# Later attention groups without selector matmuls, and one MLP chunk per batch, in an attention plus MLP kernel

## The chip, the cores and the metric

The kernel runs on one core of one Trainium2 chip. The metric is the time of one execution on the device in microseconds; before the change it is 378.05 us, the median of three runs (377.97 to 380.45). The engines are named as in the profile: PE is TensorE (PEld its weight loads), DVE is VectorE, ACT is ScalarE, POOL is GpSimd, SP is SyncE, which issues most of the DMAs.

## The reference

Eight batches of eight heads of linear attention, 576 positions of 64 numbers, feed an MLP over 4608 tokens.

```python
def phi(x):                                  # x: [b, h, 576, 64], w_phi: [64, 128]
    proj = einsum('bhsd,df->bhsf', x, w_phi)
    proj = proj - max(abs(proj), axis=-1)    # one maximum per position and head
    return concatenate([exp(proj), exp(-proj)], axis=-1)

q_p, k_p = phi(q), phi(k)
kv  = einsum('bhsf,bhsd->bhfd', k_p, v)
z   = sum(k_p, axis=2)
num = einsum('bhsf,bhfd->bhsd', q_p, kv)
den = einsum('bhsf,bhf->bhs', q_p, z) + 1e-06
x   = (num / den) transposed to [4608, 512]

h = x @ w_in                                 # [512, 2048]
g = where(h > 0, h, exp(min(h, 0)) - 1)
out = g @ w_out                              # [2048, 512], fp32
```

Because proj has its maximum m taken off before both signs, the two halves are exp(p - m) and exp(-p + m) with the same m: the first half is scaled by exp(-m), the second by exp(+m).

## The kernel before

Sixteen groups of four heads (two per batch, `n` = 0 to 15) go through the attention. For each, k and q are turned so that the 64 head dimensions lie on partitions (two pairs of heads on the two halves of 128), by PE for the first four groups and by DMA transposes afterwards. The maximum for k scales v (on POOL). The maximum for q has to come off inside the exponent, and there the positions lie along the free axis: so the maxima, found in another layout, are split into two bf16 parts, transposed on PE, and added to the projection by "selector" matmuls.

```python
def m_max(n, c):                   # maxima of |q projection|, from PSUM, on DVE
    ...
    nc.vector.tensor_reduce(mq, st["pm", n, c][:, :, 0:p1 - p0, :], axis=AX.X, op=ALU.max, ...)

def m_split(n, part):              # hi and lo parts of the maxima
    ...
    eng = nc.gpsimd if n < PE_TRANSPOSED else nc.vector
    eng.tensor_copy(hi, mq)
    eng.tensor_tensor(mhl[n % 2][:, :, NI + p[0]:NI + p[1]], mq, hi, op=ALU.subtract)

def m_pe(n, part, bank=None):      # one transpose of them
    nc.tensor.transpose(tr[:, 0, :], mhl[n % 2].rearrange("p r x -> p (r x)"), ident)

def m_copy(n, part):
    nc.vector.tensor_copy(st["mT", n], st["trm", n][:, 0:1, :])

def q_mm(n, c, bank=None):
    ...                            # the projections, w_sb against qT: 2 matmuls a piece
    for j in range(w):             # the selectors: 6 matmuls a piece
        for par in range(2):
            nc.tensor.matmul(places(par, j, 1), sel[rows, p0 + j, :], mT[rows, 0, :],
                             start=False, stop=(j == w - 1))

def q_exp(n, c, sg):               # exp(+-(p - m)) on ACT, 768 columns
    ...
def x_mm(n, part, bank=None):      # both signs accumulated in one place: num and den
    ...
        nc.tensor.matmul(pn[:, hi, x, :], Eq[:, sg, hi, par, ...], kv_sb[:, hi, pr, sg, :],
                         start=(sg == 0), stop=(sg == 1))

def x_div(n, part):
    nc.vector.tensor_scalar_add(den, pn[:, :, :, D], 1e-6)
    nc.vector.reciprocal(rec, den)
    nc.vector.tensor_tensor(xp..., pn[:, :, :, 0:D], rec..., op=ALU.mult)
```

The result is turned once more into `xT_sb`, one tile of 4608 columns that stays in SBUF, by DMA transposes from group 2 on (`x_dma`: 512 columns of whole tiles, and 64 of a mixed one per batch). The columns of two batches and their mixed tile lie one after the other, and the MLP takes them 512 at a time, nine chunks: `h_mm` (w_in against x, L510), `h_exp` on ACT (L521), `h_min` on POOL (L526), `h_elu` on DVE (L530), `o_mm` (g against w_out, L538), `o_copy` on ACT (L548), `o_store` (L554).

All eight PSUM banks are one tile; each step is told its bank. The whole program is written out as a string of letters, one per step, and is issued in that order on every engine:

```python
ORDER = """
eabefegcj7dfkA0gj7BfkBeA2CA4hBl7gl6Bmj1mj0hBCM6iBkkA2DCBFEl1NDA4Bl0EmBOCFP1BEA6QBmS2CEM0CTU4eNDB
... (22 more lines)
"""
STEPS = dict(
    c=(selectors, [()]), d=(selectors2, [()]), e=(load k), f=(load q), g=(load v),
    j=(t_pe k), k=(t_copy k), l=(t_pe q), m=(t_copy q), n=(t_dma k), o=(t_dma q),
    A=(k_mm), B=(k_exp), C=(k_max), D=(v_exp), E=(v_scale), F=(v_ones),
    M=(m_mm), N=(m_max), O=(m_split), P=(m_pe), Q=(m_copy), S=(q_mm), T=(q_exp),
    U=(kv_mm), V=(kv_copy), W=(x_mm), X=(x_div), Y=(x_pe), Z=(x_copy), z=(x_dma),
    p=(h_mm), q=(h_exp), r=(h_min), s=(h_elu), t=(o_mm), u=(o_copy), v=(o_store))   # arguments cut
```

Of the kernel before, what the change touches and what calls it, by code (L numbers as in the profile page):

```python
# [10 lines left out]
FP32 = mybir.dt.float32  # L11
# [7 lines left out]
eabefegcj7dfkA0gj7BfkBeA2CA4hBl7gl6Bmj1mj0hBCM6iBkkA2DCBFEl1NDA4Bl0EmBOCFP1BEA6QBmS2CEM0CTU4eNDB  # L19
EUTOEM6VM0DP3NW4EQNM6S2NM0OTFENU6TXP1FOUQS2VP5Y4Tj1ZS6QTl0W4mTS2kTj0XTW6TkS4XA0Tj3BY2ZA6Tkl2Bp3m  # L20
Y5BCqBZrA0p4sCM2qp5rNM6qDrBNp3l2sqp7BmrsqM4rp6NFp2qsqrp5srp4CqOqrP7l3srW0sgQmp6sEj7XqS2DTrEkM0p5
NY7qTsrS0sFp4EZTsM2M6TNp5EqNS0qrp3Trp2sOsTA6fp4CqU0qrrUBssVqA2Bp5rW0sBP7p6Xqnt4qrBrsp1QCp5zqp7qr
sp0qrszW2DsrqFsS5rEp1sTXp7qp0Trfsp3qA1rtBesqp7ECoqp6qtDrBrsp5rzsqEp0sqS1qztTrrsFTsp7EU5uS1qrUrTs
A3Vt0TCtsBW1oW5BXp7A3qtCzrtsBXzt7BnM1A5M3NBtuCztDFNEM0BztNgM2uvt6ODENP7M0nM4QNES2tTNFTfS0S4TEA2t
CTp7TTU0UBA4VtBCp1qorBW2sqp0vBOXrp7quP5p4rzQsDqFW2sqrzp6XrA0qEp5szBsp3rqCvp7rqseBp4vsrqp6DsrqS0s
rM2Tp5NFEqp7sqrp3qrsTp4rsqsM0qA5rt2CEp7NBrtsBsM0qS5NtrTEsTS0U3oTA5UCTtVBt7OnBP4W0QuS3XvW5TtDXzTE
tztfFA0EuzS2M4Bt6NTztCTS4BM2otDTEtzTFA0Eut7CntNgBA4BM2CtNtBBA0OU2CUDuP6p5VQM2qM6Np4rNEp3qBsW6rqp
2sBrp5XqFeW0qsrzS6DXrp4TEzTp3sqEsvM0S6Np2TFnEqS0Tp5rqrsU6qzrUsTrp4TzOsp3qVorA0qsA6p2Brsvsp5qCP4r
p3qQCBrp4qsW0qrst2DXBEp5BFsW0zrqtEszXS6rtTvsM0A3NtBnTt5CztDBFEM0S6zNM3TtENTU0guA3S6UTotVBvt2BtTC
p1OA3qW6urp0XBP5tBQztqCzS5uA3t7DCTEntsDBFtrBEsW1TtXEA3uM5ep0NzBEp7Cqvp6rBFsM1qp5NqrM3qrS0Np2Trsf  # L30
p4qsTp7rqOsp6qrsP5rS0qQsU2oTrUsTS4Vvp7TsW0TzS2qXA4p6rBgTzp1Cqt0svqrTp7rszDW2sBEp6Xqp5rqzstrqsrA1
S3M6EsTotCFtNDt5BEtBETM6U1NFA3UBM6VtuNBvW0tCnXA6M2Bt4NBtCW0tODXuEp7vP6EA0QM2BtzNfqp6Cuzrp5BzS2qM
0Dt4rNTzFtETssvS0EU2TS6qtFoOTrtTesUTA0nVp5uCW2zqP7p6BXrvgp4BQsqzS2qA0rp7CTrzp5sqBsrp6Dsp4BEqM0qp
7NrTrsW0qsqA2rp5BXEp6BsFqp1rCqrp4sDrqsS2rp7sTEsqA5t0BrTtCFEqU1sBrUA3sS5BtVoTCtTzA1Bt7CuzW3DBEtXn
BtEDM0M2zFNW4EtXFt6nEuNM0U4vOM2NUP7tNtQVS0M2S4TNp7TOtTt3TqS0A4rop2BTtCvTtszqA0BrtCzup7sDBzp6qW4r
qvp2uXEBp3rqszA0qM4rsp7FNzrp6qECvp5sBrp4sqsp2qrDrqP7p3Qsqrp7BsrsqS5qA0srp4Brst2EqsBp3FTECp7qtrTr
sqtsrM0U4sUNA6tBVM0BS3Nt5CtODtTFEW0uP7TtEQXS2uA6t4TzCtBzW0BtXDTFtEzW0uEp7XzS2U4TzUTS0Vvt6qTrS2vT
p5Tzp4TW0qp3XqrtrqszW0rp7Xzp2qszp1rsqtsrqzsp5rsvp7sp4p3tp2uqp1vqrqt6rsqp0rsqrsqtrsqp7rsrsp5qsp4r
qsp3rqstrqsp7rstqp5rsp4qp7rqst3rqsp5rstqtrstp7t5qp4rsp2qtrqsp7rsp4qtrqsp2rstqp7rsp4qut2ruvsqp6rv
tqsutrvstt7ttp6p5qtrqsp4rst6qtrsp5tqp4rsp3qp5rqsp1rqsutrqvsut4ruvsttvtt7p6p5qtrqsup3rvstqp6rstp5  # L40
uqp4vqrp7qrsp3rsqst6rqstrsttt7utvttt6utvttt7utvttuv
# [4 lines left out]
def kernel(  # L46
# [34 lines left out]

    consts = ctx.enter_context(tc.tile_pool(name="consts", bufs=1))
# [5 lines left out]
    moep = ctx.enter_context(tc.tile_pool(name="moep", bufs=2))  # L88
    epool = ctx.enter_context(tc.tile_pool(name="epool", bufs=4))
# [24 lines left out]
    xT_sb = consts.tile([P, N_CT, NTOK], BF16)  # L114
    FULL = 4 * P

    def full_col(b):
        return (b // 2) * 2 * S + (b % 2) * (FULL + P)

    def mixed_col(b):  # L120
        return (b // 2) * 2 * S + FULL + (b % 2) * D

    def out_rows(tile_index):
        bp, t = divmod(tile_index, 9)
        rows = []
        for half in range(2):
            if t == 4:
                b, s = 2 * bp + half, 8
            else:
                b, t4 = (2 * bp, t) if t < 4 else (2 * bp + 1, t - 5)  # L130
                s = 4 * (t4 // 2) + t4 % 2 + 2 * half
            rows.append(
                out[b * S:(b + 1) * S, :].rearrange("(p s) c -> s p c", s=NS)[s]
            )
        return rows
# [11 lines left out]
    PIECES = (((0, 4), (4, 7), (7, 9)), ((0, 3), (3, 6), (6, 9)))  # L147
    TILES = (
# [56 lines left out]


# [12 lines left out]
    def t_copy(name, n, j0, j1):  # L219
        nc.vector.tensor_copy(  # L220
            get((name + "T", n), new_t(name))[:, j0:j1, :],
            st["tr", name, n, j0][:, 0:j1 - j0, :],
        )

    def t_dma(name, n):
        nat = st[name, n // 2][:, 2 * (n % 2):2 * (n % 2) + 2]
        nc.sync.dma_start_transpose(
            out=get((name + "T", n), new_t(name)),
            in_=nat.rearrange("p r s d -> p (r s d)"),
        )  # L230
# [56 lines left out]
    def m_mm(n, c, bank=None):  # L287
        own = min(n // FIRST, 1)
        p0, p1 = PIECES[own][c]
        pj = two_banks(bank).rearrange("p r (i f) -> p r i f", f=F)  # L290
        for j in range(p1 - p0):
            for par in range(2):
                rows = slice(par * D, (par + 1) * D)
                nc.tensor.matmul(  # L294
                    pj[:, par, j, :],
                    st["qT", n][rows, PLACE_OF[own][par][p0 + j], :],
                    w_sb[rows, :],
                    start=True,
                    stop=True,
                )  # L300
        st["pm", n, c] = pj

    def m_max(n, c):
        p0, p1 = PIECES[min(n // FIRST, 1)][c]
        if n < FIRST and c == 0:

            mq = st["pm", n, c][:, 0, 0, 0:2 * p1].rearrange("p (r i) -> p r i", r=2)
            st["mq0", n] = mq
        else:
            mq = get(("mq", n), lambda: small.tile([P, 2, NI], FP32, name="mq"))  # L310
            mq = mq[:, :, p0:p1]
        nc.vector.tensor_reduce(  # L312
            mq, st["pm", n, c][:, :, 0:p1 - p0, :], axis=AX.X, op=ALU.max,
            apply_absolute_value=True,
        )

    def m_split(n, part):
        if n < FIRST:
            p = ((0, 4), (4, NI))[part]
        else:  # L320
            p = (0, NI)
        hi = mhl[n % 2][:, :, p[0]:p[1]]
        if n < FIRST and part == 0:
            mq, eng = st["mq0", n], nc.vector
        else:
            mq = st["mq", n][:, :, p[0]:p[1]]
            eng = nc.gpsimd if n < PE_TRANSPOSED else nc.vector
        eng.tensor_copy(hi, mq)  # L328
        eng.tensor_tensor(
            mhl[n % 2][:, :, NI + p[0]:NI + p[1]], mq, hi, op=ALU.subtract  # L330
        )
# [6 lines left out]
    def m_copy(n, part):  # L338
        st["mT", n] = tpool.tile([P, 1, P], BF16, name="mT")
        nc.vector.tensor_copy(st["mT", n], st["trm", n][:, 0:1, :])  # L340


    def q_mm(n, c, bank=None):
# [3 lines left out]
        qT, mT = st["qT", n], st["mT", n]  # L347
# [17 lines left out]
        for x in range(max(len(r) for r in runs)):  # L365
            for par in range(2):
                if x >= len(runs[par]):
                    continue
                j, i, m = runs[par][x]
                rows = slice(par * D, (par + 1) * D)  # L370
                nc.tensor.matmul(  # L371
                    places(par, j, m),
                    w_sb[rows, :],
                    qT[rows, i:i + m, :].rearrange("p i (h t) -> p h i t", h=2),
                    start=(x == 0),
                    stop=False,
                )
        for j in range(w):
            for par in range(2):
# [4 lines left out]
                    mT[rows, 0, :],  # L384
# [32 lines left out]
    def kv_copy(n):  # L417
        st["kv", n] = work.tile([P, 2, 2, 2, D + 1], BF16, name="kv_sb")
        nc.vector.tensor_copy(
# [10 lines left out]
    def x_mm(n, part, bank=None):  # L430
        Eq, kv_sb = st["Eq", n], st["kv", n]
        parts = x_parts(n, part)
# [30 lines left out]

    def x_pe(n, part, bank=None):
# [8 lines left out]
    def x_copy(n, part):  # L473
# [3 lines left out]
        c0 = full_col(b) + part * 2 * P  # L477
        nc.vector.tensor_copy(
            xT_sb[:, 2 * g:2 * g + 2, c0:c0 + 2 * P].rearrange(
# [4 lines left out]
        if part == 1:  # L484
            nc.vector.tensor_copy(
                xT_sb[:, 2 * g:2 * g + 2, mixed_col(b):mixed_col(b) + D],
# [3 lines left out]
    def x_dma(n, pr, mixed):  # L490
        b, g = divmod(n, 2)
        xp, ct = st["xp", n, pr], 2 * g + pr
        if not mixed:
            nc.sync.dma_start_transpose(
                out=xT_sb[:, ct, full_col(b):full_col(b) + FULL].rearrange(
# [4 lines left out]
        else:  # L500
            nc.sync.dma_start_transpose(
                out=xT_sb[:, ct, mixed_col(b):mixed_col(b) + D].unsqueeze(1),
# [4 lines left out]
    def h_mm(ch, jt, h0, h1, bank=None):  # L507
        ph = psum[:, bank, h0:h1]
        for ct in range(N_CT):
# [3 lines left out]
                xT_sb[:, ct, ch * CHUNK + h0:ch * CHUNK + h1],  # L513
# [32 lines left out]
    def o_copy(ch, tt):  # L546
        st["o", ch, tt] = opool.tile([P, DM], FP32, name="o_sb")
        nc.scalar.copy(st["o", ch, tt], st["po", ch, tt])  # L548

    def o_store(ch, tt):  # L550
        last = (ch, tt) == o_tiles[-1]
        for half, rows in enumerate(out_rows(ch * (CHUNK // P) + tt)):
            queue = nc.scalar if last and half == 0 else nc.sync
            queue.dma_start(out=rows, in_=st["o", ch, tt][half * D:(half + 1) * D])  # L554

# [17 lines left out]
    def blocks(name, n):  # L573
# [3 lines left out]
    m_parts = groups((0,), first=EACH)  # L577
# [31 lines left out]
        W=(x_mm, groups(*PAIR, first=EACH)), X=(x_div, groups(*PAIR, first=EACH)),  # L609
# [9 lines left out]
    for letter, bank in re.findall(r"([A-Za-z])(\d?)", "".join(ORDER.split())):  # L619
        fn, args = queues[letter]  # L620
        fn(*next(args), **({"bank": int(bank)} if bank else {}))
    assert all(next(args, None) is None for _, args in queues.values())

# [29 lines left out]
```

## Time and profile before

| what | value |
|---|---|
| time, median of 3 runs | 378.05 us |
| span of the profiled run | 377.5 us |
| share of the chain that ended last, PE | 81% |
| share of the chain, DVE / POOL / issue | 7% / 5% / 4% |
| L538 and L510, the two MLP products, in the chain | 31% and 30% |
| L381, the selector matmuls, in the chain | about 2% |
| POOL, share of the span | 51% |
| mean DMA rate | 105 GB/s |

The page has one row per kind of instruction, with its count, its time in total and the mean of one; an instruction is known by its line, its engine and the tiles it writes and reads (`banks` is PSUM, `e_sb`, `gT` and `o_sb` belong to the MLP, `EK`, `Eq`, `vs`, `mq`, `mhl`, `mT`, `xp` to the attention). Releasers behind an arrow name what ended a wait. The kernel has three parts: up to about 60 us the first batches fill the pipeline, from there to about 290 us attention and MLP are interleaved, and after that only the MLP is left.

### The profile page before, as it was taken

To read this page: it belongs to the slowest core of one execution; us is meant where nothing else is said; L and a number is where in the kernel's file an instruction comes from. 1 tells how busy PE (TensorE), PEld (TensorE's weight loads), DVE (VectorE), ACT (ScalarE), POOL (GpSimd) and SP (SyncE) were. 2 spreads that over 40 slices of the span, in tenths; PEclk is the share of its full clock that TensorE was granted. 3 is DMA by queue.
4 is the path that set the end of the run, shared out by engine and by line. 5 is a ranking of instruction groups with operands and counts; after the bars stand their busy time and mean duration, and the time that the engine had idled before them with its cause. 6 is when DMAs were issued, how large, how long until landed. Compare 5 with 4: busy or idle time off the path is not lost.

```text
span 377.5 us, 9991 instructions
## 1 busy us (share of the span) xinstructions
PE 349.3 (93%) x4034; PEld 193.1 (51%) x4084; DVE 249.0 (66%) x441; ACT 248.3 (66%) x453; POOL 192.3 (51%) x301
## 2 busy tenths in 40 slices
PE   2777899969999999999999999999999999999995
PEld 1665676625455555544655544644555444444442
DVE  3988986794984789658868687748754473523320
ACT  3867688648887698678965898298666453514521
POOL 8851869261954396528563575518552363413310
PEclk9899999998999999999999999999999999999999
DMA  7999988799558967478984991733014300123213
GB/s 115 202 212 209 207 124 130 96 152 141 102 77 131 157 113 104 95 137 136 151 128 94 184 168 38 118 76 76 2 23 84 76 13 0 36 50 76 63 38 76
DMA packets 68158, 39.72 MB, mean 105 GB/s; under 512 B 48016, under 2 KB 62480, under 8 KB 68112
## 3 DMA queue, kind: packets, MB, share of 16 engines
q0 software_dynamic: 15856, 18.35, 31.9%
q1 hardware_dynamic: 52176, 20.59, 31.4%
q8 instruction: 32, 0.52, 0.6%
q10 hardware_dynamic: 80, 0.13, 0.1%
q14 instruction: 14, 0.11, 0.1%
HBM read 36.77 MB, written 9.44 MB: 122 GB/s over the span
## 4 chain that ended last, share of the span: by engine, by line
PE 81%; DVE 7%; POOL 5%; issue 4%; ACT 1%; DMA 1%; SPq 0%; POOLq 0%; ACTq 0%; DVEq 0%
PE banks L538 31%; PE banks L510 30%; PE banks L439 5%; PE banks L409 5%; PE banks L238 3%; PE banks L371 3%; POOL e_sb L526 2%; PE banks L294 2%; DVE mq L312 2%; PE banks L381 2%; POOL vs L275 2%; DVE mk L256 1%; DVE mhl L328 1%; DMA e_sb<-in_w_phi_dram 1%; DVE gT L530 1%
## 5 line engine op out<-in xcount | busy, mean ns | idle before, releaser
L526 POOL TENSOR_SCALAR e_sb<-e_sb 128x512 f32<-128x512 f32 (+1 forms) x160 | 90.0, 570 | 126.1 <-ACT e_sb L521 118.9
L510 PE MATMUL banks<-xT_sb,w_in_sb 128*128 128x512 bf16 (+1 forms) x620 | 137.4, 357 | 2.2 <-issue 0.6
L538 PE MATMUL banks<-w_out_sb,gT 128*128 128x512 bf16 x546 | 133.2, 381 | 3.3 <-issue 2.4
L530 DVE SCALAR_TENSOR_TENSOR gT<-e_sb,banks 128x512 bf16<-128x512 f32 (+1 forms) x160 | 96.7, 630 | 48.8 <-POOL e_sb L526 48.3
L521 ACT ACTIVATE e_sb<-banks 128x512 f32<-128x512 f32 (+1 forms) x160 | 87.2, 561 | 48.9 <-PE banks L510 41.9
L249 ACT ACTIVATE EK<-banks 128x768 bf16<-128x768 f32 x96 | 75.1, 813 | 22.2 <-PE banks L238 14.7
L393 ACT ACTIVATE Eq<-banks 128x768 bf16<-128x768 f32 (+2 forms) x96 | 73.9, 815 | 23.6 <-PE banks L381 22.9
L510 PEld LDWEIGHTS <-w_in_sb 128*128 128x128 bf16 x640 | 58.8, 98 | 59.5 <-issue 2.3
L275 POOL TENSOR_TENSOR vs<-vn,em 128x576 bf16<-128x576 bf16 x64 | 73.2, 1153 | 23.0 <-ACT em L266 22.7
L538 PEld LDWEIGHTS <-gT 128*128 128x128 bf16 x576 | 52.7, 98 | 60.4 <-issue 0.7
L256 DVE TENSOR_REDUCE mk<-banks 128x6 f32<-128x768 f32 x48 | 45.7, 954 | 15.3 <-PE banks L238 8.0
L312 DVE TENSOR_REDUCE mq<-banks 128x6 f32<-128x768 f32 (+1 forms) x46 | 42.5, 941 | 11.9 <-PE banks L294 10.2
L548 ACT COPY o_sb<-banks 128x512 f32<-128x512 f32 x36 | 21.0, 591 | 25.8 <-PE banks L538 18.9
L456 DVE TENSOR_TENSOR xp<-banks,rec 128x640 bf16<-128x640 f32 (+2 forms) x32 | 26.4, 824 | 1.1
L439 PEld LDWEIGHTS <-Eq 128*128 128x128 bf16 x640 | 23.7, 97 | 6.1 <-issue 0.9
L439 PE MATMUL banks<-kv_sb,Eq 128*128 128x65 bf16 x640 | 25.1, 194 | 0.3 <-DVE mq L312 0.2
L409 PE MATMUL banks<-vs,EK 64*128 64x65 bf16 x1152 | 23.2, 194 | 1.0 <-DVE mq L312 0.6
L409 PEld LDWEIGHTS <-EK 64*128 64x128 bf16 x1152 | 21.0, 96 | 4.1 <-issue 1.7
L238 PE MATMUL banks<-w_sb,kT 64*128 64x128 bf16 x288 | 16.6, 225 | 4.0 <-DVE kT L220 2.4
L294 PE MATMUL banks<-w_sb,qT 64*128 64x128 bf16 x288 | 16.4, 223 | 1.3 <-DVE xp L456 0.7
L371 PE MATMUL banks<-qT,w_sb 64*128 64x384 bf16 (+2 forms) x102 | 16.6, 331 | 0.9 <-DVE mq L312 0.4
L381 PE MATMUL banks<-mT,sel 64*128 64x128 bf16 x288 | 16.6, 223 | 0.0
(45 smaller groups left out, 157.2 us busy)
## 6 DMA issues: line engine op xcount, KB each, us to landing
out_dram<-o_sb SPq DMA_DIRECT2D x71, 128.0 KB, 2.5
qn<-in_q_dram POOLq DMA_DIRECT2D x7, 576.0 KB, 7.2
kn<-in_k_dram POOLq DMA_DIRECT2D x7, 576.0 KB, 7.8
vn<-in_v_dram POOLq DMA_DIRECT2D x7, 576.0 KB, 6.8
w_in_sb<-in_moe_w_in_dram POOLq DMA_DIRECT2D x2, 1024.0 KB, 20.2
w_out_sb<-in_moe_w_out_dram POOLq DMA_DIRECT2D x1, 2048.0 KB, 32.2
xT_sb<-xp SPq DMA_TRANSPOSE x56, 2.4
qn<-in_q_dram POOLq DMA_DIRECT2D x2, 288.0 KB, 6.1
```

The costliest lines, as they stand in the source:

```text
L249: nc.scalar.activation(EK[:, sg, 6 * c:6 * c + 6, :].rearrange("p (i r) f -> p r i f", r=2), st["pk", n, c], ACT.Exp, scale=1.0 - 2.0 * sg,)
L256: nc.vector.tensor_reduce(mk[:, 6 * c:6 * c + 6].rearrange("p (i r) -> p r i", r=2), st["pk", n, c], axis=AX.X, op=ALU.max, apply_absolute ...
L275: nc.gpsimd.tensor_tensor(get(("vs", n), new_vs)[:, sg, r, 0:D], st["v", n // 2][:, 2 * (n % 2) + pr], st["em", n][:, sg, r].unsqueeze(2). ...
L312: nc.vector.tensor_reduce(mq, st["pm", n, c][:, :, 0:p1 - p0, :], axis=AX.X, op=ALU.max, apply_absolute_value=True,)
L393: nc.scalar.activation(Eq[:, sg, :, :, p0 * D:p1 * D].rearrange("p h r x -> p r h x"), st["pq", n, c][:, :, 0:(p1 - p0) * P].rearrange("p ...
L409: nc.tensor.matmul(kv[:, hi, pr, sg, :], EK[rows, sg, pr * NS + s, :], vs[rows, sg, pr * NS + s, :], start=(s == 0), stop=(s == NS - 1),)
L439: nc.tensor.matmul(pn[:, hi, x, :], Eq[:, sg, hi, par, i0 * D:(i0 + 2) * D], kv_sb[:, hi, pr, sg, :], start=(sg == 0), stop=(sg == 1),)
L510: nc.tensor.matmul(ph, w_in_sb[:, ct, jt * P:(jt + 1) * P], xT_sb[:, ct, ch * CHUNK + h0:ch * CHUNK + h1], start=(ct == 0), stop=(ct == N_ ...
L521: nc.scalar.activation(e_sb, st["ph", ch, jt, h0], ACT.Exp)
L526: nc.gpsimd.tensor_scalar(e_sb, e_sb, 1.0, 0.0, op0=ALU.min, op1=ALU.max)
L530: nc.vector.scalar_tensor_tensor(gT[:, jt, h0:h1], st["e", ch, jt, h0], -1.0, st["ph", ch, jt, h0], op0=ALU.add, op1=ALU.max,)
L538: nc.tensor.matmul(po, st["gT", ch][:, jt, tt * P:(tt + 1) * P], w_out_sb[:, jt, :], start=(jt == 0), stop=(jt == N_JT - 1),)
```

## The change

For groups 6 to 15 (`JOINED = 6`) the maximum is no longer taken off inside the exponent. The exponentials are of plus and minus the plain projection; the two signs' products with kv go to two banks instead of being accumulated, and are joined afterwards on DVE with weights that depend on the maximum alone. With both parts multiplied by exp(m), the positive one needs no factor, the negative one exp(2m), and the 1e-6 of the denominator exp(m). In that layout a position lies on a partition, so the maximum needs no transpose: the selectors, the split, the transpose and its copy fall away. Joining takes new steps: `m_exp` (letter w, ACT), `x_join` (x, DVE), `x_rec` (R, DVE), `x_scale` (y, POOL, or DVE where starred). The DMA transpose of q for these groups is done in two halves, one per head of a pair, so that a tile's 128 positions of one head lie together.

A chunk of the MLP is now one batch's whole tiles (512 columns), kept in a ring of four tiles instead of one long one; the mixed tiles of all eight batches make the ninth chunk, in a tile of its own. The string of letters is a new one, with a star behind a letter that sends the step to the other engine (DVE to ACT for copies out of PSUM, ACT to DVE for output copies, POOL to DVE or back for the split and the scaling). It is meant to leave more room behind every DMA transpose.

```diff
 ORDER = """
-eabefegcj7dfkA0gj7BfkBeA2CA4hBl7gl6Bmj1mj0hBCM6iBkkA2DCBFEl1NDA4Bl0EmBOCFP1BEA6QBmS2CEM0CTU4eNDB
+eabeeffj7k*gj6fA0kgBcA2dj7BeA4kBChl7Bhl6mBj1Cl7BkA2mDCM0Bl6ENBA4BECDm*FOA2ECm*P1Q*CBES6M0DTU4FNE
... (all lines are new)
-    xT_sb = consts.tile([P, N_CT, NTOK], BF16)
+    xT_last = consts.tile([P, N_CT, CHUNK], BF16)
+    def xT_of(ch):                                   # RING = 4
+        if ch == N_CHUNK - 1: return xT_last
+        return get(("xT", ch), lambda: xtp.tile([P, N_CT, CHUNK], BF16, name="xT"))
+    def copy_on(scalar):
+        return nc.scalar.copy if scalar else nc.vector.tensor_copy
...
     def t_dma(name, n):
+        if name == "q" and n >= JOINED:
+            for hi in range(2):
+                nc.sync.dma_start_transpose(out=out_t[:, hi], in_=nat[hi * D:(hi + 1) * D]...)
+            return
...
     def m_mm(n, c, bank=None):
+        if n >= JOINED:                              # M_PIECES = ((0, 4), (4, 7), (7, 10))
+            for v in range(v0, v1):
+                for par in range(2):
+                    nc.tensor.matmul(pj[:, par, v - v0, :], by_head(n)[rows, hi, i0 * D:(i0 + 2) * D],
+                                     w_sb[rows, :], start=True, stop=True)
...
+    def m_exp(n):                                    # exp(m) and exp(2m), 20 columns each
+        for j in range(2):
+            nc.scalar.activation(st["e1", n][:, j]..., st["mq", n]..., ACT.Exp, scale=1.0 + j)
...
     def q_mm(n, c, bank=None):
-                    stop=False,
+                    stop=n >= JOINED,
-        for j in range(w):
+        for j in range(w if n < JOINED else 0):      # the selectors
...
     def x_mm(n, part, bank=None):
+        if n >= JOINED:                              # N_PIECES = ((0, 7), (7, 14), (14, 20))
+            for v in range(v0, v1):
+                for sg in range(2):
+                    nc.tensor.matmul(pn[:, sg, v - v0, :], Eq[:, sg, hi, par, i0 * D:(i0 + 2) * D],
+                                     kv_sb[:, hi, pr, sg, :], start=True, stop=True)
...
+    def x_join(n, part):                             # 7 x 65 columns
+        nc.vector.tensor_tensor(xs, pn[:, 1], st["e1", n][:, 1, v0:v1]...to_broadcast(...), op=ALU.mult)
+        nc.vector.tensor_tensor(xs, pn[:, 0], xs, op=ALU.add)
+    def x_rec(n, part):
+        nc.vector.scalar_tensor_tensor(den, st["e1", n][:, 0, v0:v1], 1e-6, st["xs", n, part][:, :, D],
+                                       op0=ALU.mult, op1=ALU.add)
+        nc.vector.reciprocal(st["rec", n, part], den)
+    def x_scale(n, part, other=False):
+        (nc.vector if other else nc.gpsimd).tensor_tensor(xp[:, v0:v1], st["xs", n, part][:, :, 0:D],
+                                                          st["rec", n, part]..., op=ALU.mult)
...
-    def o_copy(ch, tt):
+    def o_copy(ch, tt, other=False):
-        nc.scalar.copy(st["o", ch, tt], st["po", ch, tt])
+        copy_on(not other)(st["o", ch, tt], st["po", ch, tt])
...
-            eng = nc.gpsimd if n < PE_TRANSPOSED else nc.vector
+            eng = nc.gpsimd if (n < PE_TRANSPOSED) != other else nc.vector
```

`t_copy`, `m_copy`, `kv_copy` and `x_copy` take the star in the same way. The starred steps are 17 output copies, 10 kv copies, 7 copies of transposed k and q, 6 copies of maxima, 4 splits, 4 scalings and 2 copies of x.

## The prediction

> **What bounds the kernel now.** I read the busy times first, then the same by stages of 20 us, then PE's own timeline, and last the waits of the stage where PE falls behind.
>
> ```profile
> PE 349.3 (93%) x4034; PEld 193.1 (51%) x4084; DVE 249.0 (66%) x441; ACT 248.3 (66%) x453; POOL 192.3 (51%) x301
> 0.00:20.00 20.00, 11.04 (x184) 8.44 (x185) 13.63 (x27) 12.78 (x23) 17.60 (x28) 0.91 0.99 162
> 20.00:40.00 20.00, 15.26 (x290) 11.80 (x290) 16.78 (x36) 13.40 (x25) 6.05 (x15) 1.00 1.18 209
> 80.00:100.00 20.00, 17.17 (x215) 9.50 (x219) 14.71 (x26) 13.48 (x23) 9.21 (x14) 0.91 0.92 131
> 160.00:180.00 20.00, 19.58 (x166) 9.67 (x169) 14.24 (x25) 16.26 (x30) 10.70 (x16) 1.00 0.79 132
> ```
>
> After the window and its length come the busy times of PE, PEld, DVE, ACT and POOL, then the granted clock, the DMA share and GB/s. From 100 us on PE is busy for 19.5 of every 20 us; before that it is not. Matmuls overlap, so I don't take busy time for work: I read the distance from one start to the next where PE runs without a gap.
>
> ```profile
> 242.43 0.74 PE L409 MATMUL banks<-vs,EK 64*128 64x65 bf16 x36
> ...
> 244.99 0.34 PE L371 MATMUL banks<-qT,w_sb 64*128 64x384 bf16 x2
> 245.16 0.33 PE L381 MATMUL banks<-mT,sel 64*128 64x128 bf16 x6
> 245.33 0.33 PE L294 MATMUL banks<-w_sb,qT 64*128 64x128 bf16 x6
> ...
> 254.79 0.79 PE L439 MATMUL banks<-kv_sb,Eq 128*128 128x65 bf16 x20
> 255.42 1.89 PE L510 MATMUL banks<-xT_sb,w_in_sb 128*128 128x512 bf16 x7
> ```
>
> Six selector matmuls (L381) hold PE for 245.33 - 245.16 = 0.17 us, 28 ns each; six of L294 the same; two of L371 0.17 us (82 ns each over all sizes); twenty of L439 0.63 us (31 ns); L409 16 ns. The MLP's 512-column matmuls follow each other at 216 ns (four in 0.86 us in the chain), the 256-column ones at half of that. A transpose is about 60 to 70 ns.
>
> PE's work is then: first MLP product 512 x 216 + 128 x 108 ns = 124.4 us; second 576 x 216 = 124.4; L439 640 x 31.4 = 20.1; L409 1152 x 15.9 = 18.3; L238, L294, L381 864 x 28.4 = 24.5; L371 8.4; 110 transposes 6.8. Sum 326.9 us. The span is 377.5, so 50.6 us are lost. Put against the weight loads recorded in each stage, the loss is 14.2 us in 0-20, 8.0 in 20-40, 4.7 in 40-60, 2.6 in 60-80, 4.6 in 80-100, about 10 in all from 100 to 280 (1.1 per 20 us), none from 280 to 360, 5.0 at the end (the last eviction and store). So there are two prices: a PE instruction removed after 100 us is worth nearly its full time; before 60 us the time belongs to the chain through DVE and ACT.
>
> The 4.6 us of 80-100 have one cause.
>
> ```profile
> 78.60 3.23 DVE L328 CAST mhl<-mq 128x18 bf16<-128x18 f32 x1
> 78.70 2.27 POOL L275 TENSOR_TENSOR vs<-vn,em 128x576 bf16<-128x576 bf16 x2
> ...
> 82.10 0.23 PE L335 MATMUL banks<-ident,mhl 128*128 128x128 bf16 x1 [2.62 <-DVE mhl L329]
> ```
>
> ```profile
> 78.00:84.00 6.00, 3.14 (x35) 1.57 (x35) 5.93 (x7) 1.24 (x4) 5.00 (x6) 0.99 0.91 140
> 84.00:90.00 6.00, 5.67 (x110) 3.27 (x108) 1.73 (x2) 5.45 (x9) 0.00 (x0) 0.72 1.72 165
> ```
>
> The reader is to see a copy of 18 columns that takes 3.23 us beside two GpSimd multiplies (the median of the twelve such copies is 0.18 us), PE idle for 2.6 us behind it, and then a clock of 0.72 for 6 us, which is 1.7 us more.
>
> [...] three more of the twelve took 0.55 to 0.82 us. [...] The trace's divisions (L456: 692, 824, 957 ns for 512, 640, 768 elements) give 162 + 1.036 N ns[...], and they read PSUM, as the new ones will.
>
> **The change, part by part.** Ten of the sixteen groups (n = 6 to 15) become selector-free.
>
> PE: 180 selector matmuls go, 180 x 28.4 ns = 5.1 us; ten transposes of the maxima go, 0.7 us; the maxima are now taken per pair of tiles and head, 20 projections a group instead of 18, +20 x 28.4 ns = 0.6 us. The 40 products with kv per group stay 40, in three pieces rather than two, each sign in a bank of its own. Net -5.2 us. These groups run mostly after 90 us, where PE is full, so I count all of it.
>
> DVE per joined group: gone are two divisions of 824 + 216 + 165 ns (2.41 us), the split (0.36 at the medians) and the copy of the maxima (0.22). New are the joins: two passes over 455 columns at 634 ns, twice, and two over 390 at 566 ns, 3.67 us; three small pairs at about 0.39 us (by the rows for `den` and `rec`), 1.17 us; and one larger maximum (1.22 instead of 0.95), 0.27 us. Net 5.1 - 3.0 = +2.1 us, +21 us in ten groups. The stars of the order move work both ways: 17 output copies come to DVE (about +11 us), 4 scalings (+2), while 10 kv copies (-7), 7 transposed copies (-3), 6 copies of maxima (-1) and 2 of x (-1) go to ACT. In all 249 + 22 = 271 us, 73% of a span near 371. In the stretch from 100 to 240 us, where DVE is at 15.2 of 20 us, it comes to about 17.3.
>
> ACT: -17 x 0.59 us output copies, +20 exponentials of 20 columns at 0.21 us, +10 kv copies and 15 small ones, about +13 us together: 248 + 7 = 255.
>
> POOL: 26 scalings. From the rows of L275 and L329 (1153 ns for 576 elements, 219 for 18) I estimate 1.67 ns per element + 190 ns, about 0.9 us each: +23 us, 192 to 215, 58%.
>
> DMA: the q transposes of these groups are two halves, 22 instead of 12; none of the transposes shows as a wait of PE today. The ring of four x tiles saves SBUF and asks that chunk b is read before batch b+4 writes: by the letters of the order, 91 us of PE work lie between, so it waits for nothing. Room between the last transpose of a batch and the first matmul of its chunk is 6.7 to 9.1 us of PE work now, against 3.8 to 10.4 before, with a landing of 2.4 us on the page: safe before, safer now, and no time by itself.
>
> Order: the splits change engine. Group 4's, the one of 78.60, goes to POOL, and its room between last maximum and first use grows from 2.3 to 4.2 us of PE work. I expect most of that stall gone: 2.6 us of waiting and 1.7 us of clock, less what such a place loses anyway, -3.5 us. At the start the first copy of kT goes to ACT and the 1.35 us that build the selectors on DVE move behind it, about -0.5 us. DVE work ahead of the first MLP matmul falls from 25.2 to 22.1 us by count, ACT's stays at 22.7; but up to the last of chunk 0 ACT's count rises from 56.7 to 67.5 us while PE does 4.2 us more, so I take no more from the first 60 us.
>
> New waits: 30 small operations with two SBUF inputs each can be blocked by POOL as the casts were. The twelve casts lost 0.37 us on average (mean 551 ns, median 180), 0.13 without the long one: 4 to 11 us of DVE time in a stretch 86% full. Only what exceeds the 2 to 3 us of room at a bank reaches PE: +2 us.
>
> Sum: -5.2 - 3.5 - 0.5 + 2.0 = -7.2; 378.05 - 7.2 = 370.9, said as 371.
>
> **The rivals.** First, DVE takes PE's place: joins, output copies and blocked small operations fill it past 90%, banks come free late, and PE loses 2 us in every 20 instead of 1.1. For it: 86% by count, all in a fixed order. Against it: ACT stood at 16.3 of 20 us in 160-180 without hurting PE, and the joined groups no longer have the chain maximum, split, transpose, copy in front of their exponentials. It would make 376 to 380. Second, the removal counts and the stall merely moves: another blocked operation idles PE once more and the clock falls again; then only the 5.2 us stay, 373 to 374. Third, the start shortens, since DVE bounds it (16.8 and 18.4 of 20 us in the second and third stage) and 3 us of its work go: another 2 to 3 us, 367 to 369.
>
> **Range and chances.** The PE term is the sure one (5.2, 1.4%). The stall term is worth 0 to 4, the start -2 to +3, the new waits 0 to 8. Together 365.5 to 377.5. The line of 2% is 370.5, almost at my number, so faster by over 2% and within 2% get nearly equal chances, and slower needs the first rival at its worst: 0.45, 0.49, 0.06.
>
> **What would show it.** Right: no selector or `mhl` rows after about 100 us but for group 5; PE's work 321.7 us by the same sum; no stage after 60 us with a clock under 0.95; 1 to 1.4 us lost per 20 us from 100 to 280; joins of about 0.63 us; DVE 265 to 280, POOL 210 to 220. Wrong: waits of PE for the joins or for gT of 0.5 us and more, small operations with a mean above 0.8 us, a clock dip anywhere after 60 us, waits for a transpose, or a chunk 0 that ends later.

## The result, and the profile after

The kernel after takes 369.13 us (median of 4 runs, 369.07 to 369.67) against 378.9 us for the kernel before on the same chip: ratio 0.9741, 95% interval 0.9701 to 0.9781. A later set of runs gave 368.96 us and 0.9726 (0.9712 to 0.9741). The prediction was 371 us, 365.5 to 377.5, with 0.45 on faster by over 2%.

The busy times and three stages of 20 us of the kernel after, with the columns as before (PE, PEld, DVE, ACT, POOL, granted clock, DMA share, GB/s):

```profile
PE 345.5 (94%) x3867; PEld 188.5 (51%) x3914; DVE 267.1 (73%) x470; ACT 253.4 (69%) x482; POOL 214.7 (58%) x323
20.00:40.00 20.00, 17.14 (x321) 13.71 (x316) 17.06 (x36) 17.66 (x34) 8.98 (x18) 1.00 1.18 210
80.00:100.00 20.00, 19.74 (x226) 10.51 (x222) 15.34 (x28) 16.95 (x32) 13.23 (x22) 1.00 1.06 163
160.00:180.00 20.00, 19.79 (x204) 9.70 (x207) 16.57 (x30) 14.56 (x26) 14.72 (x22) 1.00 1.10 164
```

PE does less and is fuller; DVE, ACT and POOL have all become busier, as counted (271, 255 and 215 us were expected). The stage of 80 to 100 us no longer has a hole or a low clock, and in 20 to 40 us both PE and ACT are busier. The new operations in the groups of the kernel after, and the removed ones that are left:

```profile
L555 DVE TENSOR_TENSOR xs<-banks,e 128x455 f32<-128x455 f32 x20 | 12.5, 623 | 8.4 <-PE banks L510 6.1 <-ACT e L377 1.5 <-POOL xj L576 0.3
L560 DVE TENSOR_TENSOR xs<-banks,xs 128x455 f32<-128x455 f32 x20 | 12.6, 632 | 0.7
L576 POOL TENSOR_TENSOR xj<-xs,recj 128x448 bf16<-128x448 f32 x17 | 15.9, 935 | 6.1 <-DVE recj L571 6.1
L671 DVE COPY o_sb<-banks 128x512 f32<-128x512 f32 x17 | 11.6, 684 | 9.9 <-PE banks L661 9.9
L449 PE MATMUL banks<-mT,sel 64*128 64x128 bf16 x108 | 6.4, 223 | 0.0
```

The joins take 0.62 to 0.63 us where 0.634 was worked out, the scalings 0.935 where about 0.94 was; 180 of 288 selector matmuls are gone. PE's work by the sum of the prediction is 321.7 us, 5.2 less. Subtracting it stage by stage as there gives what PE loses (the stretch from 100 to 280 us is counted as one window here):

| stage, us | lost before | lost after |
|---|---|---|
| 0-20 | 14.2 | 14.4 |
| 20-80 | 15.3 | 11.8 |
| 80-100 | 4.6 | 0.6 |
| 100-280 | 11.1 | 13.3 |
| 280 to the end | 4.5 | 4.6 |

The span falls from 377.5 to 367.3 us: 5.2 us of work, 4.0 in the stage of the stall, 3.5 in 20 to 80 us, and 2.2 given back from 100 to 280 us; the first and the last row give back another 0.3. The rows of each column add up to 0.9 us less than span minus work, since a matmul on the edge of two stages is counted in both. Some 0.5 us of the 15.3 belongs to the stall, because PE's wait of 2.62 us began at 79.5: kernels with the same steps up to there, in the experiments below, lose 14.9 to 15.1 us from 20 to 80 us. The experiments ask who is behind each of these.

### The profile page after: what moved, and what is told of

The parts are those of the page before. It is cut to its first block, busy times and chain, and to the rows that moved or that the text cites. A ratio compares the mean times of both kernels' runs of the same rounds, so it can differ in the third digit from the quotient of the medians.

```text
span 367.3 us, 9751 instructions
## 1 busy us (share of the span) xinstructions
PE 345.5 (94%) x3867; PEld 188.5 (51%) x3914; DVE 267.1 (73%) x470; ACT 253.4 (69%) x482; POOL 214.7 (58%) x323
## 4 chain that ended last, share of the span: by engine, by line
PE 80%; DVE 7%; ACT 4%; POOL 3%; issue 3%; DMA 2%; SPq 0%; POOLq 0%; DVEq 0%; ACTq 0%
PE banks L661 32%; PE banks L633 30%; PE banks L477 5%; PE banks L510 3%; PE banks L437 2%; PE banks L267 2%; PE banks L326 2%; DMA qn<-in_q_dram 2%; PE banks L526 2%; DVE gT L653 1%; ACT EK L278 1%; POOL vs L304 1%; POOL e_sb L649 1%; DVE mk L285 1%; ACT e_sb L644 1%
## 5 line engine op out<-in xcount | busy, mean ns | idle before, releaser
L644 ACT ACTIVATE e_sb<-banks 128x512 f32<-128x512 f32 (+1 forms) x160 | 88.4, 563 | 62.3 <-PE banks L633 54.4
L633 PE MATMUL banks<-xT,w_in_sb 128*128 128x512 bf16 (+1 forms) x557 | 122.7, 355 | 2.0 <-DVE mq L368 0.5
L354 DVE TENSOR_REDUCE mx<-banks 128x6 f32<-128x768 f32 (+1 forms) x30 | 30.9, 1040 | 6.0 <-PE banks L326 5.3
L576 POOL TENSOR_TENSOR xj<-xs,recj 128x448 bf16<-128x448 f32 (+1 forms) x26 | 23.3, 897 | 9.3 <-DVE recj L571 9.3
L555 DVE TENSOR_TENSOR xs<-banks,e 128x455 f32<-128x455 f32 (+1 forms) x30 | 18.0, 600 | 8.9 <-PE banks L510 6.6
L671 ACT COPY o_sb<-banks 128x512 f32<-128x512 f32 x19 | 11.1, 589 | 14.8 <-DMA out_dram<-o_sb 13.2
L510 PEld LDWEIGHTS <-Eq 128*128 128x128 bf16 x400 | 16.2, 97 | 7.3 <-issue 1.1
L560 DVE TENSOR_TENSOR xs<-banks,xs 128x455 f32<-128x455 f32 (+1 forms) x30 | 18.3, 610 | 1.1
L671 DVE COPY o_sb<-banks 128x512 f32<-128x512 f32 x17 | 11.6, 684 | 9.9 <-PE banks L661 9.9
L510 PE MATMUL banks<-kv_sb,Eq 128*128 128x65 bf16 x400 | 17.1, 194 | 0.3 <-DVE mx L354 0.3
```

The costliest lines, as they stand in the source:

```text
L354: nc.vector.tensor_reduce(mq.rearrange("p (v r) -> p r v", r=2)[:, :, v0:v1], st["pm", n, c][:, :, 0:v1 - v0, :], axis=AX.X, op=ALU.max, a ...
L510: nc.tensor.matmul(pn[:, sg, v - v0, :], Eq[:, sg, hi, par, i0 * D:(i0 + 2) * D], kv_sb[:, hi, pr, sg, :], start=True, stop=True,)
L633: nc.tensor.matmul(ph, w_in_sb[:, ct, jt * P:(jt + 1) * P], xT_of(ch)[:, ct, h0:h1], start=(ct == 0), stop=(ct == N_CT - 1),)
L644: nc.scalar.activation(e_sb, st["ph", ch, jt, h0], ACT.Exp)
```

## The experiments

The theory: PE's work sets the time after 100 us, so removed matmuls count; one stall of a small DVE copy behind GpSimd costs the 80 to 100 us stage its 4 us; the start is the chain through DVE and ACT. Against it stand the rival that DVE takes PE's place, and, for the stall and the start, that the new order does it, whatever engine the steps run on.

Each ratio is against the kernel before, run beside the kernel in question: its median was 379.53 us for four kernels built on it (the split alone, the maximum, the later load, the ring), 378.69 us for four built on the kernel after (the zeros, the split back on DVE, the copies back on DVE, the output copies on ACT), and 379.5 us for the rest. Differences from the kernel after are taken from 369.13 us, or in the rest from 368.96 us.

### Is PE the limit where the selectors were?

```diff
 # kernel after, q_mm of groups 6 to 15
-        for j in range(w if n < JOINED else 0):
+        for j in range(w):
...
+                    zeros[rows, :] if n >= JOINED else st["mT", n][rows, 0, :],
```

> Kernel after, with the 180 selector matmuls of groups 6 to 15 put back as matmuls against a tile of zeros (same shapes and places, nothing added to the result, none of the split, transpose or copy). If PE's work sets the time there: +5.1 us on the kernel after, 374 to 374.5. If those groups are bound by DVE and ACT, PE has room for them: +2 us or less, 371 or less.

Measured: 373.2 us (372.91 to 373.66), ratio 0.9841 (0.9807 to 0.9875), so +4.1 us on the kernel after; span 371.3. The 180 matmuls are worth 23 ns each of the 28 that they hold PE. From 100 to 280 us PE's loss falls from 13.3 to 12.4 us: about a microsecond of them fills time in which PE would have stood. The rival of +2 us or less falls. The selectors are four tenths of the gain of 9.8 us. The zeros put back PE's work alone; what the split, the transpose and its copy cost beside it is not tested.

### The stall at 78 us

In the kernel before, GpSimd's multiplies beside the slow copy (78.60 to 81.83) stand between the issues of two loads:

```profile
77.84 0.83 POOL L192 DMA_DIRECT2D vn<-in_v_dram  x1
...
80.91 0.26 POOL L284 CAST vs<-em 128x18 bf16<-128x18 f32 x1
81.04 0.80 POOL L192 DMA_DIRECT2D qn<-in_q_dram  x1
```

The twelve copies of this kind on DVE in that trace are slow only beside GpSimd: the four of 0.55 us and more each meet its instructions and end within 0.05 us of the end of one, and the eight of 0.17 to 0.18 us meet none. Four kernels ask what of this counts. First, group 4's split moved to POOL in the kernel before:

```diff
-            eng = nc.gpsimd if n < PE_TRANSPOSED else nc.vector
+            eng = nc.gpsimd if n < PE_TRANSPOSED + 1 else nc.vector
```

> Kernel before, with only group 4's split of the maxima on POOL instead of DVE. If the stall of 78 to 90 us comes from one copy on DVE that GpSimd keeps out, PE loses about 0.6 us there instead of 2.6 and the clock stays up: -3 to -4 us, about 374.5 to 375.5, and the clock of 84 to 90 us at 1.00. If the stall only moves to POOL, behind its own multiplies: -1 us or nothing, and a wait of PE for mhl of 1.5 us or more.

Measured: 376.25 us, ratio 0.9913 (0.989 to 0.9936), a gain of 3.3 us, inside the 3 to 4 of the first expectation (its 374.5 to 375.5 us is missed, because the kernel before ran at 379.5 and not at 378.5 beside it). The loss from 80 to 100 us falls from 4.6 to 1.6 us. The windows and PE's next wait for data in this kernel:

```profile
78.00:84.00 6.00, 5.77 (x65) 2.98 (x66) 5.04 (x7) 4.08 (x9) 5.89 (x9) 1.00 0.94 147
84.00:90.00 6.00, 5.23 (x113) 3.27 (x113) 2.90 (x8) 4.64 (x8) 0.76 (x3) 1.00 1.20 199
```

```profile
85.14 0.39 PE L510 MATMUL banks<-xT_sb,w_in_sb 128*128 128x512 bf16 x1 [0.61 <-DMA xT_sb<-xp]
```

PE is busy for 5.77 of 6 us where it was for 3.14, and the clock stays at 1.00; but PE now comes to the second chunk early and waits 0.61 us for a DMA transpose, which the kernel before never does. This is what room behind a transpose is for.

Second, the same copy made by a maximum over an axis of one element, which, like the copy, has one input in SBUF:

```diff
-        eng.tensor_copy(hi, mq)
+        if n == PE_TRANSPOSED:
+            nc.vector.tensor_reduce(hi, mq.unsqueeze(3), axis=AX.X, op=ALU.max)
+        else:
+            eng.tensor_copy(hi, mq)
```

> Kernel before, with group 4's copy of the maxima made by a maximum over an axis of one element, an operation with one input in SBUF[...]. If copies[...] are what GpSimd blocks, this operation takes under 0.25 us at the same place; the subtraction behind it has two inputs in SBUF and is then either blocked in its turn (1 to 3 us, no gain) or not (0.2 us, gain 3 to 4 us). If the small copy was slow for another reason, the new operation takes 3 us too.

Measured: 379.1 us, ratio 0.9984 (0.9969 to 0.9998), no gain worth the name. The timeline of DVE and of POOL at that place:

```profile
79.10 0.18 DVE L329 TENSOR_REDUCE mhl<-mq 128x18 bf16<-128x18 f32 x1
79.31 2.86 DVE L332 TENSOR_TENSOR mhl<-mq,mhl 128x18 bf16<-128x18 f32 x1
```

```profile
78.35 0.83 POOL L192 DMA_DIRECT2D vn<-in_v_dram  x1
79.20 2.27 POOL L275 TENSOR_TENSOR vs<-vn,em 128x576 bf16<-128x576 bf16 x2
81.41 0.26 POOL L284 CAST vs<-em 128x18 bf16<-128x18 f32 x1
81.55 0.80 POOL L192 DMA_DIRECT2D qn<-in_q_dram  x1
```

The maximum takes 0.18 us at the place where the copy took 3.23 (each starts 0.10 us before the two multiplies), and the subtraction behind it, which has two inputs in SBUF, takes 2.86 instead of 0.18. At this place the kind of operation decides: the cast is held off (3.23 us), the reduction that starts at the same point is not (0.18 us), and the subtraction behind it is (2.86 us). It waited through two multiplies, a cast and part of the issue of a load (79.31 to 82.17). PE's wait behind the subtraction, and the clock after it:

```profile
82.23 0.23 PE L338 MATMUL banks<-ident,mhl 128*128 128x128 bf16 x1 [2.24 <-DVE mhl L332]
84.00:90.00 6.00, 5.68 (x115) 3.46 (x116) 3.03 (x5) 5.91 (x9) 0.00 (x1) 1.00 1.66 149
```

The clock does not fall here. The profiled run is one of the shorter ones, 378.17 us, with a mean clock of 0.999; in 18 of the 20 runs the mean clock was 0.986 to 0.994, so it may well have fallen in them.

Third, the load that POOL issues in front of these multiplies moved some 3 us later:

```diff
-... z t N g M2 u v t6 O D E N P7 M0 n M4 Q N E S2 t T N F T f
+... z t N M2 u v t6 O D E N P7 M0 n M4 Q N E S2 t T N F g T f
```

> Kernel before, with one load of v issued by POOL some 3 us later, so that no load stands in front of group 4's copy of the maxima. If it is the issue of the load that lets GpSimd hold the copy off for 3.2 us, the copy takes under 0.7 us and the kernel gains 2.5 to 4 us. If the two multiplies hold it off, the copy still takes 1 to 3 us and the gain is under 2 us.

Measured: 376.52 us, ratio 0.9917 (0.9896 to 0.9938), a gain of 3.0 us, the first expectation. The copy, the subtraction and POOL's string beside them:

```profile
78.86 0.45 DVE L328 CAST mhl<-mq 128x18 bf16<-128x18 f32 x1
79.34 1.16 DVE L329 TENSOR_TENSOR mhl<-mq,mhl 128x18 bf16<-128x18 f32 x1
```

```profile
77.01 3.45 POOL L275 TENSOR_TENSOR vs<-vn,em 128x576 bf16<-128x576 bf16 x3
80.40 0.27 POOL L284 CAST vs<-em 128x18 bf16<-128x18 f32 x1
```

Each of the two now waits for one multiply only: the copy ends at 79.31, two thirds through the three multiplies, the subtraction at 80.50, at their end. With the load out of the way DVE gets in between two GpSimd instructions; with it in front, it did not in three kernels (3.23, 2.86, and 3.23 us in the kernel with the ring below). Why moving the load makes the difference isn't shown, nor whether it is the load or what its moving did to the string behind it.

Fourth, the other way round: the kernel after with this split back on DVE (one star less in its order).

```diff
-... M0 A5 C t O* B E N P4 ...
+... M0 A5 C t O B E N P4 ...
```

> Kernel after, with only group 4's split of the maxima back on DVE. If the engine of this split is what removed the stall: +2 to +4 us, with a DVE copy of 1 us or more and a clock under 0.9 behind it. If the new order alone has moved the copy away from GpSimd's multiplies: within 0.7 us of the kernel after.

Measured: 369.79 us, ratio 0.9754 (0.9718 to 0.979), +0.7 us, the second expectation, with intervals that overlap the kernel after's. The copy meets a multiply and ends with it (76.31 against 76.27):

```profile
75.72 0.59 DVE L394 CAST mhl<-mq 128x18 bf16<-128x18 f32 x1
76.35 0.18 DVE L395 TENSOR_TENSOR mhl<-mq,mhl 128x18 bf16<-128x18 f32 x1
```

```profile
74.25 0.83 POOL L201 DMA_DIRECT2D qn<-in_q_dram  x1
75.11 1.16 POOL L304 TENSOR_TENSOR vs<-vn,em 128x576 bf16<-128x576 bf16 x1
76.20 0.81 POOL L201 DMA_DIRECT2D qn<-in_q_dram  x1
```

Either engine is good here: the new order alone had removed all of the stall but the 0.60 us that PE waits. Here a load stands in front too, and the copy waits for one multiply, so a load in front is not enough to be held off for longer. But this copy comes 0.6 us into its multiply; the operations that were held through several came within 0.15 us of the end of the load's issue. Whether that matters was not tried.

### The ring, alone and with the split

In the kernel before, in its own order, `xT_sb`, `full_col` and `mixed_col` replaced by `xT_of` and `xT_last`:

```diff
-                xT_sb[:, ct, ch * CHUNK + h0:ch * CHUNK + h1],
+                xT_of(ch)[:, ct, h0:h1],
```

> Kernel before, in its own order, with only the MLP's chunks changed: one batch's whole tiles per chunk in a ring of four tiles, the mixed tiles of all batches in the last chunk. If the ring saves space and no time: within 1 us of before. If the chunks that straddle two batches cost waits today, or if the ring makes a transpose wait for a chunk: a change of 2 us or more either way.

Measured: 379.37 us, ratio 0.9992 (0.9971 to 1.0013). No time by itself, and the stall is as before: the copy takes 3.23 us, PE waits 2.61 us behind it, and the clock drops in both windows.

```profile
79.10 3.23 DVE L327 CAST mhl<-mq 128x18 bf16<-128x18 f32 x1
78.00:84.00 6.00, 3.33 (x34) 1.83 (x33) 5.93 (x7) 0.97 (x4) 5.50 (x7) 0.86 0.96 144
84.00:90.00 6.00, 5.84 (x117) 3.17 (x114) 2.22 (x3) 5.07 (x8) 0.00 (x0) 0.86 1.66 146
```

Then with the split on POOL as well:

> Kernel before with group 4's split on POOL and the batch-wise chunks in a ring together. With the split alone PE comes sooner to the second chunk and waits 0.61 us there for the transpose of a mixed tile, which the batch-wise chunk doesn't need. If that is the room that the new chunks give: 0.5 to 0.7 us less than with the split alone, 375.6 to 375.8, and no wait for a transpose. If not: the same as the split alone.

Measured: 375.45 us, ratio 0.9893 (0.9878 to 0.9908), 0.8 us less than with the split alone by the medians of two sets of runs; the intervals of the two ratios overlap. The wait for a transpose is gone: after 83 us PE's only recorded gaps up to 92 us are these.

```profile
83.06 0.81 PE L537 MATMUL banks<-w_out_sb,gT 128*128 128x512 bf16 x3 [0.16 <-issue]
86.32 0.81 PE L537 MATMUL banks<-w_out_sb,gT 128*128 128x512 bf16 x3 [0.16 <-issue]
```

The loss from 80 to 100 us is 0.7 us, where the split alone left 1.6. So the batch-wise chunks do buy room; the trace shows the wait gone, and 0.8 us of time is likely but not clear of the two intervals.

### The start

```diff
 # kernel after, stars taken from: k x3, m x4, Z x2, Q x4 and V x3 of the first groups
-eabeeffj7k*gj6fA0kgBcA2dj7BeA4kBChl7Bhl6mBj1Cl7BkA2mDCM0Bl6ENBA4BECDm*FOA2ECm*P1Q*CBES6...
+eabeeffj7kgj6fA0kgBcA2dj7BeA4kBChl7Bhl6mBj1Cl7BkA2mDCM0Bl6ENBA4BECDmFOA2ECmP1QCBES6...
```

> Kernel after, with the 16 copies out of PSUM that the first groups send to ACT back on DVE (7 of turned k and q, 4 of maxima, 2 of x, 3 of kv). If these copies are why PE loses 3.5 us less in the first 80 us: +2.5 to +4 us, 371.5 to 373. If it is the order of the steps: under +1.2 us.

Measured: 371.21 us, ratio 0.9789 (0.9756 to 0.9823), +2.1 us, between the two expectations. PE's waits show two that the kernel after does not have (columns: total, times, longest):

```profile
PE banks L437 <- DVE qT L232: 0.9, 1, 0.9
PE banks L633 <- DVE mT L406: 0.8, 1, 0.8
```

The copies sent to ACT are worth 2.1 us in all, but not all of it where the start gained. By the same subtraction PE loses 13.3 us from 20 to 80 us in this kernel, against 11.8 in the kernel after and 15.3 in the one before: about 1.5 of the 3.5 us are the copies'. Another half a microsecond lies before 20 us, where the wait of 0.9 stands (at 17.5 us), and as much from 80 to 100 us. The other 2 us of the 3.5 are left for the new order by elimination; no run tests a part of it. If DVE's load as such were the limit, taking another 1.35 us off it there should help as well:

```diff
-        nc.vector.tensor_scalar(sel, ...)      # selectors2; its letter d now stands behind the second h
+        nc.gpsimd.tensor_scalar(sel, ...)
```

> Kernel after, with the 1.35 us that spread the selectors out moved from DVE to POOL, behind the loads of w_in, where POOL waits some 3.8 us for v. If the chain through DVE sets the start (DVE is busy without a gap from 7 to 30 us): -0.7 to -1.4 us, 367.7 to 368.4. If the loads or ACT set it: within 0.4 us of the kernel after.

Measured: 369.29 us, ratio 0.9735 (0.972 to 0.975), against 368.96 and 0.9726 of the kernel after beside it: nothing. DVE, nearly without a gap from 7 to 30 us (0.43 us is the longest in the kernel after), is not the limit there by its sum. What the kernel above adds are single waits of PE for copies.

> The kernel after, unchanged, for comparison on the same chip as the next three: 369 us.

Measured: 368.96 us (368.81 to 369.33).

### Does DVE take PE's place?

```diff
-... u* ...
+... u ...                      # 17 times
```

> Kernel after, with all 36 output copies on ACT as before. ACT goes from 253 to about 264 us of busy time and DVE from 267 to 255. If PE alone sets the time from 100 us on: within 1 us of the kernel after. If the balance of DVE and ACT mattered: +2 us or more, with waits of PE behind ACT.

Measured: 369.46 us, ratio 0.9746 (0.9705 to 0.9787): the balance of the output copies is worth nothing in this kernel. The other direction:

```diff
 def x_join(n, part):
-        nc.vector.tensor_tensor(xs, pn[:, 1], ..., op=ALU.mult)
+        for _ in range(2):
+            nc.vector.tensor_tensor(xs, pn[:, 1], ..., op=ALU.mult)
```

> Kernel after, with the first pass of every join done twice (30 passes of 0.55 to 0.63 us more on DVE, same result), +18 us of DVE time in the stretch where it is fullest. If DVE still has room beside PE: +2 us or less. If DVE is about to take PE's place: +6 us or more, with waits of PE for banks behind DVE.

Measured: 380.7 us (380.54 to 381.05), ratio 1.0042 (1.0018 to 1.0065): 17 us more of DVE (283.7 against 266.5 us of busy time) cost 11.7 us, and the whole gain is gone. PE's waits in this kernel, and its busy times in two stages:

```profile
PE banks L437 <- DVE xs L561: 1.7, 2, 1.3
...
PE banks L267 <- DVE mx L354: 1.3, 1, 1.3
PE banks L634 <- DVE gT L654: 0.8, 3, 0.3
PE banks L510 <- DVE xs L561: 0.8, 2, 0.6
PE banks L267 <- DVE gT L654: 0.7, 3, 0.3
```

```profile
140.00:160.00 20.00, 17.57 (x228) 9.22 (x230) 17.47 (x29) 16.35 (x31) 10.72 (x14) 1.00 0.51 77
200.00:220.00 20.00, 17.93 (x211) 9.21 (x211) 17.39 (x32) 13.12 (x24) 10.15 (x15) 1.00 0.69 117
```

PE's loss from 100 to 280 us rises from 13.3 to 22.8 us, with DVE only at 17.4 of 20; some 2 us more are lost after 280 us. The rival is right about this distance from the kernel after, not about the kernel after itself, which has next to none of these waits. The busy share does not tell the two apart: in its fullest stage the kernel after has more on DVE, and PE is full.

```profile
240.00:260.00 20.00, 19.89 (x144) 9.06 (x144) 18.06 (x30) 15.43 (x29) 11.65 (x18) 1.00 0.49 98
```

The second pass also holds the two banks of a piece some 0.6 us longer; whether the sum of DVE's work or the bank costs the 11.7 us, this kernel does not separate.

## Why the prediction was right, step by step

The number was 371 and came out 369.1. A gain of 7.2 us was worked out, and 9.8 came (378.9 to 369.1); nearly all of the difference is the start. By terms:

- **Selectors, -5.1 us, all of it on PE.** Right in kind: putting the matmuls back costs 4.1 us. About one microsecond of theirs lies in time that PE would have lost.
- **The stall, -3.5 us.** The cause was right (the stage went from 4.6 to 0.6 us lost, and in the kernel before the split alone gives 3.3), the agent only half right: the prediction named two, group 4's split going to POOL and more room in front of its use, and did not weigh them. With the split back on DVE the kernel after loses only 0.7 us. The order had already moved the copy to a place where it waits for one multiply. The move of engine is a second way to the same end.
- **The start, -0.5 us.** The mis-sized term: 3.5 us came between 20 and 80 us (about 3 without the part of the stall). I had seen DVE's count fall by 3 us and ACT's rise by 11 and let them cancel. Sums did not size the start here: 16 copies on the other engine are worth 1.5 us in this stretch, 2.1 in all, and 1.35 us off DVE's sum are worth nothing. What gives the other 1.5 to 2 us stays open. The third rival, 2 to 3 us more at the start, is the one that came about, though the reason it gave, less work on DVE as a sum, is not borne out.
- **New waits, +2 us.** The size was right (+2.2 us from 100 to 280 us), by luck: the mechanism was not. That the 30 small operations with two SBUF inputs can be blocked as the casts were was an estimate (the twelve subtractions with two inputs in SBUF of the kernel before, L329, took 0.18 us each). They hardly were: in the kernel after

```profile
L567 DVE SCALAR_TENSOR_TENSOR denj<-e,xs x30: 155/168/595, 126.3 to 294.3; 128x7 f32<-128x7 f32 x20, 128x6 f32<-128x6 f32 x10
```

  (minimum, median and longest in ns) the longest took 0.60 us and the median 0.17. The 2.2 us are not in PE's recorded waits either; part of it is time that the selectors used to fill, as the zeros showed (0.9 us), and the rest is not settled.
- **Ring and room.** Right that the ring is worth nothing by itself, and right that room isn't where the time was; the first wait for a transpose came when the stall was taken away in the kernel before, and the ring removed it.
- **The first rival**, DVE in PE's place, did not come about, but lay closer than 0.06 for slower suggests: with one pass of the joins doubled, 6% more busy time on DVE, the gain is gone. From 100 to 240 us DVE stood at 16.8 of 20 us (117.4 of 140), where 17.3 had been counted; the kernel with the doubled pass stands at 17.3 (121.3 of 140).

## What to carry to other kernels

Price a removed matmul at its start-to-start distance in the stage where it runs, and only if PE is full there; here 23 of 28 ns came back. In a fixed order, look for the small copies that take many times their median beside GpSimd: moving the load in front (3.0 us) or their engine (3.3 us) was worth nearly the same here, and a new order had the same effect. The busy share of an engine beside a full PE does not say how much more it can take (18.1 of 20 us did no harm in one kernel, 17.4 came with a loss in another): test the distance by doubling one operation before moving more work to it.

## What the runs showed of the hardware

- DVE operations that GpSimd kept out waited through several GpSimd instructions (3.23 and 2.86 us, through two multiplies, a cast and all or part of the issue of a load) or for one (0.45, 0.59 and 1.16 us). What decides between the two was not found.
- The clock fell behind 2.6 us of PE's idle time in two profiled runs (0.72 in one window of 6 us in the kernel before, 0.86 in each of two with the ring) and stayed at 1.00 behind 2.24 us in one (the kernel with the maximum). Whether the length of the idle time or chance decides is not shown.
- On DVE a multiplication of 455 columns in PSUM by weights in SBUF, one weight for 65 columns (623 ns), and an addition of 455 columns in PSUM to 455 in SBUF (632 ns) cost nearly the same.
